# Order of the last half products, the layer sums and the turns at the end of a round, in an RWKV-6 attention with a two-layer SiLU network

## Chip, cores and metric

The kernel runs on one core of one Trainium2 chip. The metric is the device time of one execution in microseconds; lower is better.

## The reference

An RWKV-6 recurrence over 768 tokens for 4 batches and 8 heads of 48 channels gives, after a change of layout, a matrix x of 3072 x 384, which passes a network of two layers with SiLU between. All is float32.

```python
for t in range(S):
    kt, vt, rt, wt = (k[:, :, t], v[:, :, t], r[:, :, t], w[:, :, t])
    cur = np.einsum('bhd,bhe->bhde', u[None] * kt, vt)
    y[:, :, t] = np.einsum('bhd,bhde->bhe', rt, state + cur)
    state = wt[:, :, :, None] * state + np.einsum('bhd,bhe->bhde', kt, vt)
...
x = np.ascontiguousarray(attn_out.transpose(0, 2, 1, 3)).reshape(B * S, H * D)
h = x @ w_in                      # 384 -> 2048
g = h * (1.0 / (1.0 + np.exp(-h)))
return (g @ w_out).astype(np.float32)
```

## The kernel before, in words

**Tiling.** Time is cut into six chunks of 128 tokens. A *unit* is one chunk of two batches, so there are twelve units, i = 0 to 11, worked on in turn. Within a chunk the recurrence is made parallel: queries and keys are multiplied by running products of w level by level (seven levels, block sizes 1 to 64), matmuls of keys and queries give a triangle of scores, and the scores times the values, plus the queries times the state at the start of the chunk, give y. Then the state is advanced.

**A manual schedule.** Every engine works through its own instructions in the order in which the program writes them, and the program interleaves three units by hand. In the loop at line 1264, iteration i (a "round") contains

- the attention of unit i (groups of steps that `mix(i)` returns),
- the first layer of unit i-1 (`ups(i-1)`, eight steps),
- the second layer of unit i-2 (`downs(i-2)`, seven steps).

The tuple `room` says how many of the fifteen layer steps are done after each group. From unit 4 on there are eleven groups, and the last two are `end[0]` and `end[1]` in `mix`.

**The first layer** (`first_layer`, line 1049; from unit 3 on, `NFAST`) is a fast scheme: fewer products of blocks of weights and of x, with sums made beforehand. It has two halves, m = 0 and 1, of the hidden features. For each half eight named products are added up in four PSUM banks, p_h (h0, h1) and p_o (o0, o1): p1, p6, p7 and p4 in one bank, one upon the other, p5 and p3 in another, p2 and n1 in a third. After each a bank is read: ScalarE copies (line 1074), VectorE adds (line 1077), ScalarE applies SiLU (line 1080, and line 1082 for p4). The SiLU of p3 is written back to a PSUM bank, from which it is read later. In `ups` the last three steps are p7, p3 and p4 of half 1, in this order; p4 is 16 matmuls (its left operands are x sums, `spare` and `x_sum`), and each matmul leaves two records in the trace.

**The second layer** (`quarter`, line 1131) is a fast scheme of seven products Q0 to Q6, each of 8 matmuls of 128 x 192, with operands that `sums` (line 1115) makes on VectorE from the hidden features: for each half m four additions or subtractions of 128 x 512 (line 1127). Two of them read the PSUM bank that holds p3's SiLU, and the fourth reads what p4's SiLU wrote. Q0 and Q1 need no sums, Q2 to Q5 do. Q0 is written to the bank that held p3's SiLU of half 0, Q1 to the one that p4 of half 1 used. Partial results are copied by ScalarE (line 1161) before the next product may use the bank.

**The end of a round.** After the last bursts of scores (line 692) ScalarE copies eight and four blocks of them from PSUM to `score` (line 792), out of the banks p_sc and p_m. Then come, in program order:

- `turn_apart` (line 805, matmuls at 811): the keys of unit i are transposed into the p_sc banks, and `turn_k` copies them to `kq` on ScalarE (line 819). Units 10 and 11 have neither this nor the update, since no state follows them.
- `y_state` (line 826, matmuls at 835 and 842): state times queries, into the p_m banks; `y_values` (line 850): values times scores, and ScalarE's copies to `yt` (line 861).
- the turns of unit i+1 (`turn`, line 346): VectorE transposes w and k (line 360, two instructions each), and POOL makes the first product of w (`product`, line 406) between them. Turn k writes the tile that `turn_apart` of unit i reads.
- `sums` of half 0 of unit i-1.
- `update` (line 888): TensorE multiplies `kq` and values (line 896), POOL scales the state (line 901), VectorE adds (line 910).

The next round begins with the turn of r (line 360), the first growth of queries and keys (`grow_own`: POOL line 643, VectorE line 616), and the moves of x: ten DMAs from `yt` to `xt` on ScalarE's queue (line 928), two ahead of the copy of Q0's partial result and eight ahead of the next. Then POOL makes the rest of w's products (line 406), two steps of the bonus (line 491, which waits for block sums of VectorE, line 525) and the key products of levels 2 and 3 (line 634), which the next burst of scores (line 692) needs. SP issues all loads, some 60 a round.

Of the kernel before, what the change touches and what calls it, by code (L numbers as in the profile page):

```python
# [38 lines left out]
def kernel(  # L39
# [29 lines left out]
    NPAIR = 4  # L69
# [225 lines left out]
    room = pt.tile([128, 4, DM // 2], F32, name="partial", bufs=1).rearrange("p x d -> p (x d)")  # L295
# [159 lines left out]
    at = 768  # L455
# [474 lines left out]
    def both(fn, i, *args):  # L930
        return [(fn, i, b, *args) for b in range(NB)]

    def block_loads(i, names="wkr"):
        return [(load_blocks, i, name, g) for name in names for g in range(4)]
# [3 lines left out]
    def mix(i):  # L938

        ahead = i + 1 < len(units)  # L940

        def at(now, *steps):
            return steps if now else ()

        def bonus_steps(j, *steps):
            return [(block_bonus, j, x) for x in steps]

        def sum_steps(j, *steps):
            return [(block_sum, j, x) for x in steps]

        def turns(j):
            return [*both(turn, j, "w"), (product, j, 0), *both(turn, j, "k")]

        def start(j):
            return [*[(product, j, l) for l in range(1, NL)], (grow_own, j, 1)]

        end = [[*at(ahead, *bonus_steps(i + 1, 0, 1, 2, 3))],
               [*at(i < len(units) - NB, (turn_apart, i), (turn_k, i)), (y_state, i), *both(y_values, i), *at(ahead, *turns(i + 1)),
                (sums, i - 1, FH // 2 - 2 if i - 1 < NFAST else 0), *both(update, i), *at(not ahead, (move_x, i))]]
        if i < NPAIR:  # L960
            groups = [[*both(turn, i, "w"), (product, i, 0)],
                      [*both(turn, i, "k"), (odd_ones, i)], [*both(turn, i, "r"), (start_levels, i), (prepare_keys, i, 1)],
                      [(prepare, i, 1), *[(product, i, l) for l in range(1, NL)]],
                      [(burst, i, 1), (keep_level, i, 1)],
                      [(keep_level, i, 2), (go_on, i, 2)],
                      [(prepare, i, 3), (reverse_v, i), (bonus, i, 0), (bonus_sum, i, 0)],
                      [(bonus, i, 1), (burst, i, 3), (keep_level, i, 3), (bonus, i, 2)],
                      [(keep_level, i, 4), (go_on, i, 4), (bonus_sum, i, 1), (load_rk, i + 1), (load_u,)],
                      [(prepare, i, 5), (make_block_mask,), (bonus_spread, i), (bonus_write, i)],
                      [(burst, i, 5), (keep_level, i, 5), (keep_level, i, 6), (go_on, i, 6)], *end]  # L970
        else:
            groups = [[*both(turn, i, "r"), (grow_own, i, 0), (move_x, i - 1, 0, 2, nc.scalar)],
                      [*start(i), *sum_steps(i, 0, 1), *bonus_steps(i, 4, 5), (move_x, i - 1, 2, None, nc.scalar)],
                      [(odd_keys, i, 2), (grow_keys, i, 2, False), (grow_queries, i, 2), *sum_steps(i, 2)],
                      [(prepare, i, 3), *bonus_steps(i, 6, 7)],
                      [(burst, i, 3), (keep_level, i, 3), *sum_steps(i, 3, 4), (block_move, i), *at(ahead, (load_rk, i + 1))],
                      [(keep_level, i, 4), (go_on, i, 4)],
                      [(prepare, i, 5), (reverse_v, i)],
                      [(block_spread, i), (block_write, i)],
                      [(burst, i, 5), (keep_level, i, 5), (keep_level, i, 6), (go_on, i, 6)], *end]  # L980

        loads = [*at(i >= NPAIR and ahead, *block_loads(i + 1, "w")), *at(i >= NPAIR - 1 and ahead, *block_loads(i + 1, "r")),
                 *at(i + NSLOT < len(units), *block_loads(i + NSLOT, "k"))]
        if i + 1 < len(units):
            loads.insert(len(loads) // 2, (load_values, i + 1))

        if i == NPAIR - 1:
            late.extend(loads[-2:])
            loads = loads[:-2]
        if i == NPAIR:  # L990
            groups[1] += late
            groups[3] += loads[:2]
            loads = loads[2:]

        behind = groups[8 if i < NPAIR else 5 if i == NPAIR else 2:][:4 if i + NSLOT >= len(units) else None]
        for at, group in enumerate(behind):
            group += loads[at * len(loads) // len(behind):(at + 1) * len(loads) // len(behind)]
        return groups
# [3 lines left out]
    FH, DH = FC // 2, DM // 2  # L1002
    NFAST = 3
# [39 lines left out]
    def keep_banks():  # L1043

        for x in range(2):
            kept[f"h{x}"] = ps.tile([128, 512], F32, name="p_h", bufs=2)
            kept[f"o{x}"] = second[0].tile([128, 512], F32, name="p_o", bufs=2)
# [124 lines left out]
    def ups(i):  # L1172

        if i >= NFAST:
            order = (((0, "p1"), (0, "p5"), (0, "p2")), ((0, "p6"), (0, "n1"), (1, "p1")), ((0, "p7"), (0, "p3")),
                     ((0, "p4"), (1, "p2"), (1, "p6")), ((1, "p5"), (1, "n1")), ((1, "p7"),), ((1, "p3"),), ((1, "p4"),))
            made = [[(first_layer, i, half, name) for half, name in step] for step in order]
            if i == len(units) - 1:
                made[6].append((sums, i, 0))
            made[-1].append((sums, i, 1))  # L1180
            return made
        steps = [[(up, i, m)] for m in range(FC // 2)]
        for m in range(FH // 2 - (1 if i == len(units) - 1 else 2)):

            steps[FH // 2 + 1 + m].append((sums, i, m))
        steps[-1].append((sums, i, FH // 2 - 1))
        return steps

    def downs(i):
        return [[(quarter, i, x)] for x in range(7)]  # L1190

    def do(*steps):
        for fn, *args in steps:
            fn(*args)
# [69 lines left out]
    for i in range(3, len(units)):  # L1264
        steps = downs(i - 2) + ups(i - 1)
        groups = mix(i)
        if i - 1 >= NFAST:
            groups[3].append((sums_of_x, i - 1))
        if i == NTOK + 1:
            groups[4].insert(1, (weight_sums, 3))  # L1270
            for which, place in enumerate((6, 8, 9)):
                groups[place].append((in_weight_sums, which))
        if i == NFAST + 1:
            keep_banks()
            steps[1].append((in_weight_sums, 3))
        room = (1, 1, 0, 2, 1, 1, 1, 1, 1, 2, 2, 1, 1) if i < NPAIR else (2, 1, 2, 2, 1, 1, 1, 2, 1, 1, 1)
        for group, count in zip(groups, room):
            do(*group)
            for step in steps[:count]:
                do(*step)  # L1280
            steps = steps[count:]
# [34 lines left out]
```

## Time and profile before

| | |
|---|---|
| median of three runs | 594.56 us |
| the three runs | 588.8, 594.56, 597.63 us |
| span of the profiled execution | 588.6 us |
| granted TensorE clock | 1.0 throughout rounds 4 to 11 |
| TensorE busy in the chain of work that ended last | 76% of the span |

In the profile PE is a matmul, PEld a load of weights, DVE VectorE, ACT ScalarE, POOL GpSimd, SPq and ACTq the queues from which DMAs are issued. "L1065" is line 1065. A row of a timeline gives start, duration, engine, line, operation, the tile written and those read, shapes, how many instructions are merged, and in brackets how long the engine stood before and what released it. Buffer numbers are left out.

### The profile page before, as it was taken

Reading aid. Unit: us, or ns where it says so; the run is one execution under the profiler, and the core shown is the slowest. Engines: PE = TensorE matmul, PEld = TensorE weight load, DVE = VectorE, ACT = ScalarE, POOL = GpSimd, SP = SyncE. Lnnn points to the kernel's source line nnn. Section 1 sums busy time; section 2 is a strip of 40 time slices with the busy share of each in tenths; the row PEclk is TensorE's granted clock in tenths of the full one; section 3 lists DMA queues with packets and bytes.
Section 4 is the critical chain, followed back from the end, with each engine's and each line's share of the span. In section 5 each row is a group of like instructions: output and inputs, shape, how many; then the busy total and the mean of one; then the engine's idle time right before and its main releaser. Section 6 shows DMA issues by size and latency. Waiting matters only on the chain.

```text
span 588.6 us, 19384 instructions
## 1 busy us (share of the span) xinstructions
PE 573.7 (97%) x8070; PEld 533.3 (91%) x8070; DVE 455.7 (77%) x703; ACT 264.2 (45%) x582; POOL 354.1 (60%) x415
## 2 busy tenths in 40 slices
PE   8989999999999999999999999999999989999997
PEld 8767876798899989999999989999999989999997
DVE  7979789998898898787788898888678797861150
ACT  5679694431531561561561561460470462370320
POOL 5989778357768478287486496485676677500000
PEclk9999999999999999999999999999999999999999
DMA  9957785343432643544543544444354460100000
GB/s 231 311 122 195 167 244 82 47 86 70 102 68 39 133 71 53 131 66 75 114 68 60 123 62 68 105 75 73 85 100 71 95 102 27 38 7 24 28 3 26
DMA packets 203383, 53.70 MB, mean 91 GB/s; under 512 B 186784, under 2 KB 195104, under 8 KB 203296
## 3 DMA queue, kind: packets, MB, share of 16 engines
q1 hardware_dynamic: 197360, 48.73, 41.0%
q10 hardware_dynamic: 5936, 3.74, 2.4%
q8 instruction: 63, 1.03, 0.8%
q14 instruction: 24, 0.20, 0.1%
HBM read 43.21 MB, written 5.24 MB: 82 GB/s over the span
## 4 chain that ended last, share of the span: by engine, by line
PE 76%; SPq 5%; DVE 5%; POOL 4%; DMA 4%; ACT 3%; issue 1%; ACTq 1%; POOLq 0%; DVEq 0%
PE p_o L1156 26%; PE p_h L1065 16%; PE p_o L1065 8%; PE p_h L1011 8%; PE p_h L1156 4%; PE p_m L1095 4%; PE p_m L856 2%; PE p_sc L692 2%; DVE score L561 2%; SPq L127 2%; PE p_m L835 2%; DMA vq<-in_v_dram 2%; ACT score L792 2%; POOL w_in_sb L259 2%; POOL tk L634 1%
## 5 line engine op out<-in xcount | busy, mean ns | idle before, releaser
L634 POOL TENSOR_TENSOR tk<-tk,tw 128x256 f32<-128x256 f32 x128 | 91.3, 734 | 42.8 <-ACT tk L604 27.6
L491 POOL TENSOR_TENSOR ruk<-tokens_rk 128x768 f32<-128x768 f32 (+1 forms) x32 | 53.6, 1687 | 70.9 <-DVE block_sums L525 36.6
L1156 PE MATMUL p_o<-own,temps 128*128 128x192 f32 x528 | 88.8, 327 | 1.3 <-ACT partial L1161 1.3
L1156 PEld LDWEIGHTS p_o<-own,temps 128*128 128x128 f32 x528 | 86.0, 190 | 2.5 <-ACT partial L1161 2.4
L1011 PE MATMUL p_h<-xt,w_in_sb 128*128 128x256 f32 x288 | 66.1, 384 | 1.7 <-POOL w_in_sb L259 1.5
L1065 PE MATMUL p_h<-xt,w_in_sb 128*64 128x128 f32 x1008 | 62.8, 274 | 0.4 <-issue 0.4
L1011 PEld LDWEIGHTS p_h<-xt,w_in_sb 128*128 128x128 f32 x288 | 53.6, 190 | 10.0 <-POOL w_in_sb L259 2.4
L1156 PE MATMUL p_o<-w_out_sb,gt 128*128 128x192 f32 x340 | 59.9, 329 | 0.2 <-DVE temps L1127 0.2
L616 DVE TENSOR_TENSOR tr<-tr,tw 128x512 f32<-128x512 f32 x61 | 57.3, 939 | 2.6 <-PE p_m L692 2.1
L1065 PEld LDWEIGHTS p_h<-xt,w_in_sb 128*64 128x64 f32 x1008 | 55.8, 137 | 2.0 <-issue 0.9
L1156 PEld LDWEIGHTS p_o<-w_out_sb,gt 128*128 128x128 f32 x340 | 55.3, 190 | 2.0 <-issue 1.2
L1161 ACT COPY partial<-p_o 128x192 f32<-128x192 f32 x33 | 10.6, 320 | 95.7 <-PE p_o L1156 46.5
L406 POOL TENSOR_TENSOR tw<-tw 128x256 f32<-128x256 f32 (+6 forms) x83 | 40.0, 482 | 17.7 <-DVE tw L360 13.8
L1065 PE MATMUL p_o<-xt,w_in_sb 128*64 128x128 f32 x720 | 46.9, 273 | 0.0
L604 ACT COPY tk<-tk 128x256 f32<-128x256 f32 x52 | 21.2, 407 | 53.8 <-POOL tk L634 49.2
L1065 PEld LDWEIGHTS p_o<-xt,w_in_sb 128*64 128x64 f32 x720 | 40.8, 137 | 0.0
L1074 ACT COPY gt<-p_h 128x512 f32<-128x512 f32 x45 | 26.2, 582 | 30.4 <-PE p_h L1065 30.4
L1080 ACT ACTIVATE gt<-gt 128x512 f32<-128x512 f32 x36 | 22.7, 631 | 34.1 <-DVE gt L1077 33.9
L710 DVE COPY_PREDICATED score<-mask,p_sc 128x512 f32<-128x512 int8 x42 | 31.3, 800 | 5.8 <-PE p_sc L692 5.5
L1077 DVE TENSOR_TENSOR gt<-p_o,gt 128x512 f32<-128x512 f32 x27 | 18.4, 683 | 19.4 <-PE p_o L1065 19.4
L1077 DVE TENSOR_TENSOR gt<-p_h,gt 128x512 f32<-128x512 f32 x27 | 18.6, 687 | 17.3 <-PE p_h L1065 16.2
L643 POOL TENSOR_TENSOR tk<-tk,tw 128x256 f32<-128x256 f32 x32 | 30.9, 986 | 0.0
(225 smaller groups left out, 1272.0 us busy)
## 6 DMA issues: line engine op xcount, KB each, us to landing
w_out_sb<-in_moe_w_in_dram SPq DMA_DIRECT2D x6, 768.0 KB, 7.1
w_out_sb<-in_moe_w_out_dram SPq DMA_DIRECT2D x4, 768.0 KB, 5.1
own<-in_moe_w_out_dram SPq DMA_DIRECT2D x4, 768.0 KB, 5.8
tokens_rk<-in_r_dram SPq DMA_DIRECT2D x8, 384.0 KB, 4.4
tokens_rk<-in_k_dram SPq DMA_DIRECT2D x8, 384.0 KB, 5.3
tokens_w<-in_w_dram SPq DMA_DIRECT2D x8, 384.0 KB, 6.4
raw<-in_w_dram SPq DMA_DIRECT2D x80, 32.0 KB, 2.3
raw<-in_k_dram SPq DMA_DIRECT2D x80, 32.0 KB, 2.1
```

The source lines that it names most:

```text
L406: engine.tensor_tensor(out=up, in0=t[:, :, 0::2], in1=t[:, :, 1::2], op=ALU.mult)
L491: mul = lambda out, one, two: nc.gpsimd.tensor_tensor(out=out, in0=one, in1=two, op=ALU.mult)
L616: nc.vector.tensor_tensor(out=odd, in0=odd, in1=tw[i][l][:, :, 0::2][:, :, :, None].to_broadcast([128, Q, L >> (l + 1), c]), op=ALU.mult)
L634: nc.gpsimd.tensor_tensor(out=out, in0=have, in1=odd_products(i, l, b, *blocks), op=ALU.mult)
L643: nc.gpsimd.tensor_tensor(out=have, in0=have, in1=odd_products(i, l, b, [2, NP * ni]), op=ALU.mult)
L710: nc.vector.copy_predicated(out=dst, mask=masks[l][:, :, None].to_broadcast([128, NB, NP, ni, c]), data=sc[e].rearrange("p (b q) (i c) -> ...
L1011: nc.tensor.matmul(p_h[:, a, :], lhsT=w_in_sb[:, c, f * 128:(f + 1) * 128], rhs=xt[i][:, c, :], start=(c == 0), stop=(c == KC - 1))
L1065: nc.tensor.matmul(p[h:h + PD, q, :], lhsT=left[:, f:f + PD], rhs=right, start=first and n == 0 and q == 0, stop=last and n == len(pairs) ...
L1074: nc.scalar.copy(out=g(*{"p1": (0, 0), "p6": (0, 1), "p5": (1, 1)}[name]), in_=p)
L1077: nc.vector.tensor_tensor(out=to, in0=p, in1=to, op=ALU.add)
L1095: nc.tensor.matmul(po[i, b], lhsT=gt[i, f // 2][:, f % 2, b * L:(b + 1) * L], rhs=w_out_sb[:, f, :], start=(f == 0), stop=(f == FC - 1))
L1156: nc.tensor.matmul(p, lhsT=left(f), rhs=right[:, f, :], start=which in (0, 1, 3) and f == 0, stop=f == FH - 1, skip_group_check=True)
```

## The change

For rounds 4 to 11 two things are moved; no instruction is added or removed.

```diff
-        end = [[*at(ahead, *bonus_steps(i + 1, 0, 1, 2, 3))],
+        end = [[*at(i > NFAST, (sums, i - 1, 0)), *at(ahead, *bonus_steps(i + 1, 0, 1, 2, 3))],
                [*at(i < len(units) - NB, (turn_apart, i), (turn_k, i)), (y_state, i), *both(y_values, i), *at(ahead, *turns(i + 1)),
-                (sums, i - 1, FH // 2 - 2 if i - 1 < NFAST else 0), *both(update, i), *at(not ahead, (move_x, i))]]
+                *at(i <= NFAST, (sums, i - 1, FH // 2 - 2)), *both(update, i), *at(not ahead, (move_x, i))]]
...
-        room = (1, 1, 0, 2, 1, 1, 1, 1, 1, 2, 2, 1, 1) if i < NPAIR else (2, 1, 2, 2, 1, 1, 1, 2, 1, 1, 1)
+        room = (1, 1, 0, 2, 1, 1, 1, 1, 1, 2, 2, 1, 1) if i < NPAIR else (2, 1, 2, 2, 1, 1, 1, 2, 1, 2, 0)
```

`sums` of half 0 goes from behind the turns to the start of `end[0]`, ahead of p3 of half 1. The last layer step, p4 of half 1 together with `sums` of half 1, which followed `end[1]`, now follows p3 directly, ahead of `end[1]`. So the order becomes, engine by engine:

| engine | before | after |
|---|---|---|
| TensorE | p3, turn of keys, state product, values, update, p4, Q0 | p3, p4, turn of keys, state product, values, update, Q0 |
| VectorE | p7's addition, p3's addition, turns of w and k, sums 0, state, sums 1, turn of r | p7's addition, sums 0, p3's addition, sums 1, turns of w and k, state, turn of r |
| ScalarE | SiLU of p7 and p3, kq, yt, SiLU of p4, moves of x | SiLU of p7, p3 and p4, kq, yt, moves of x |

The order on POOL and of SP's DMAs stays as it is. Rounds up to 3 are unchanged.

## The prediction

> **What bounds the kernel now.** I read the page's busy times first, then a table of stretches cut at the starts of the second layer's first product (Q0, line 1156), then TensorE's waits, then the timelines of single engines around two ends of rounds. "Round i" is iteration i of the loop at line 1264; the change acts in rounds 4 to 11.
>
> ```profile
> PE 573.7 (97%) x8070; PEld 533.3 (91%) x8070; DVE 455.7 (77%) x703; ACT 264.2 (45%) x582; POOL 354.1 (60%) x415
> ```
> ```profile
> 215.40:259.60 44.20, 44.20 (x723) 43.19 (x721) 36.14 (x55) 19.37 (x47) 28.18 (x35) 1.00 0.47 85
> 304.80:351.10 46.30, 45.15 (x722) 43.43 (x720) 41.13 (x57) 19.27 (x47) 31.45 (x37) 1.00 0.45 82
> ```
> The columns of the second are the stretch, its length, and the busy us of PE, PEld, DVE, ACT and POOL, then granted clock, DMA share and GB/s. The stretch from round 5's Q0 to round 6's holds TensorE solidly and is 44.20 us long at full clock; the one from round 7 to 8 has the same matmuls and 46.30. So TensorE is the bound, and all that an order can win is the difference to 44.20 (43.20 where units lack the last products): over the eight stretches 1.3 + 0 + 1.0 + 2.1 + 0 + 1.2 + 1.9 + 0 = 7.5 us, of which the end of a round is a part.
>
> ```profile
> PE p_m L835 <- ACT score L792: 2.2, 4, 1.1
> PE p_o L1156 <- ACT partial L1161: 1.3, 2, 0.8
> ```
> ```profile
> 206.31 1.04 PE L1065 MATMUL p_h<-xt,raw 128*64 128x128 f32 x16
> 208.63 0.69 PE L811 MATMUL p_sc<-ident,tk 48*128 48x48 f32 x15 [0.21 <-ACT score L792]
> 210.18 0.96 PE L835 MATMUL p_m<-tr,state 48*48 48x128 f32 x25 [0.36 <-ACT score L792]
> ```
> ```profile
> 208.60 1.52 ACT L792 COPY score<-p_m 64x256 f32<-64x256 f32 x4
> ```
> This is the end of round 4: the turn of keys (L811) and the state product (L835) wait until ScalarE has copied scores out of the banks that they write; the L792 copies end at 210.12. The table of waits shows only part of it, because pipelined matmuls hide gaps, so I take it from starts. From the start of p3 of half 1 (206.31) to Q0 (215.39) round 4 takes 9.08 us; round 5, below, takes 251.89 to 259.58 = 7.69.
>
> ```profile
> 251.89 1.04 PE L1065 MATMUL p_h<-xt,raw 128*64 128x128 f32 x16
> 253.74 0.70 PE L811 MATMUL p_sc<-ident,tk 48*128 48x48 f32 x16
> 257.72 1.06 PE L1065 MATMUL p_h<-spare,w_in_sb 128*64 128x128 f32 x16
> 259.58 2.71 PE L1156 MATMUL p_o<-w_out_sb,gt 128*128 128x192 f32 x15
> 278.13 0.69 PE L692 MATMUL p_sc<-tr,tk 48*64 48x64 f32 x32
> ```
> The same reading gives 9.08 for round 7 (342.05 to 351.13), and 7.7 to 7.8 for rounds 6, 8 and 9. Rounds 10 and 11 have no turn of keys and no update, 0.63 + 0.72 us less, so 6.34 would be undisturbed: they take 8.31 (477.46 to 485.77) and 6.70 (522.27 to 528.97). Waits at ends of rounds: 1.39 + 1.39 + 1.97 + 0.36 = 5.1 us.
>
> **The change, part by part.** No instruction is added or removed, and SP's order is the same. *TensorE:* the 16 matmuls of p4 (32 records, 257.72 to 259.58, 1.86 us) go ahead of L811. They stand where TensorE would wait, and 1.86 covers 1.39 twice and 0.36, and all but 0.1 of 1.97: a gain of 5.0. Their inputs (x sums, weights) are long ready, but they add to the bank that VectorE reads for p7 (the L1077 before p3's), a wait that the update used to cover. That read ends at 252.87 where p4 would now start at 253.74, and in round 4 at 208.10 against 208.16: nothing, but with no room.
>
> *VectorE:* the four sums of half 0 go ahead of the addition for p3 (L1077), and the four of half 1 ahead of the turns of w and k. This is where cover may go.
>
> ```profile
> 252.18 0.69 DVE L1077 TENSOR_TENSOR gt<-p_h,gt 128x512 f32<-128x512 f32 x1 [0.72 <-PE p_h L1065]
> 253.85 0.69 DVE L1077 TENSOR_TENSOR gt<-p_h,gt 128x512 f32<-128x512 f32 x1 [0.98 <-PE p_h L1065]
> 254.46 1.30 DVE L360 STREAM_TRANSPOSE tw<-raw 128x512 f32<-128x512 f32 x2
> 257.44 0.67 DVE L1127 TENSOR_TENSOR temps<-gt,p_o 128x512 f32<-128x512 f32 x1
> 258.04 1.13 DVE L1127 TENSOR_TENSOR temps<-temps,gt 128x512 f32<-128x512 f32 x1
> ```
> In round 5's frame: half 0's sums start at 252.87 and take .57 + .60 + 1.16 + 1.21 = 3.5 us beside a busy POOL, or 4 x .60 = 2.4 beside an idle one. So p3's addition runs to 256.0 to 257.1 instead of 254.5, and its SiLU on ScalarE ends at 256.7 to 257.8. Behind that SiLU on ScalarE are p4's SiLU (0.55), the two kq copies (L819, 0.86) and the yt copies. The kq copies end at 258.1 to 259.2; the update's matmuls, now due at 257.00 + 1.86 = 258.86, wait 0 to 0.3 us. I take 0.15 in rounds 5, 6, 8 and 9. In rounds 4 and 7, where ScalarE's copies are late and TensorE now is not, the same sum gives 0.55 to 0.9; I take 0.7. Together 4 x 0.15 + 2 x 0.7 = 2.0 given back. Then yt follows 2 us later (259.2 to 261.6), and the moves of x on ScalarE's queue; the first landed in the queue at 261.01 in round 6, some later because they also wait for SP's earlier loads. The second-layer partial copy behind two moves needs Q0's end anyway, so I cost this at nothing; if that cover is gone, it is 0.8 us a round, the longest such wait shown.
>
> Half 1's sums wait for p3's SiLU (257.8 at the late end), and the fourth for p4's. With POOL idle they last 2.4 us, to 260.2; the turns of w then end at 261.5 instead of 255.76, 5.7 later. Queued behind them are the turn of k, the state addition (L910), the turn of r. Waiting for them is POOL:
>
> ```profile
> 255.84 1.04 POOL L406 TENSOR_TENSOR tw<-tw 128x512 f32<-128x512 f32 x1 [0.64 <-DVE tw L360]
> 268.78 2.41 POOL L491 TENSOR_TENSOR ruk<-tokens_rk 128x384 f32<-128x384 f32 x2 [4.31 <-DVE block_sums L525]
> 273.48 3.29 POOL L634 TENSOR_TENSOR tk<-tk,tw 128x256 f32<-128x256 f32 x4
> ```
> Its run from L406 lasts without a gap from 255.84 to 264.48, 8.64 us, then stands 4.31. After the change it is 261.55 to 270.2: the slack is eaten and the bonus step (L491) starts at 270.2, 1.4 later. VectorE's block sums are not what it waits for then, as they had the sums ahead of them before and have them ahead now. From L491's start to the last key product (273.48 + 3.29 = 276.77) it is 8.0 us, so keys are ready at 278.2, and TensorE asks for them at 278.13 (L692). That is a wait of 0.1 to 0.3, or none if half 0's sums take 2.4. I take 0.15 in each of the 7 rounds 5 to 11: 1.0 us. Bounds: 0, and 1.2 a round (8.4) should both sets of sums run at the slow rate.
>
> A rule speaks against this change. The Trainium skill, "TensorE: Matmul & The Clock Gate", section "Architectural detail", says that VectorE and ScalarE are strictly first in, first out. By it the turns pay every microsecond that a sum waits for ScalarE, as in my sum; without it the 5.7 us would be nothing. No row of this trace shows a turn passing a waiting sum.
>
> The sum: -5.0 + 2.0 + 1.0 = -2.0 us. The profiled span of 588.6 would be 586.6. The three runs have 588.8 to 597.63 and a median of 594.56, 6 us above the span: I carry the difference over and say **592.5**.
>
> **Rivals.** *All of it is kept* (chance 0.18): the sums run at 0.60 us each, nothing waits behind them, and the whole 5.0 us shows: 589.5. For: POOL stands 4.31 us. Against: its end leaves 1.4 us before L692. Even with every wait of the eight stretches gone it is 594.56 - 7.5 = 587.1, so being faster by over 2% (about what a measurement of this kernel can tell from no change: 11.9 us) needs something that no row shows: 0.02.
>
> *Slower: the keys become the bound at L692* (0.18). If the turns of w are 2 us later than I say (sums at 3.5 us twice, 2.2, on a late SiLU), the keys are at 280.2 in round 6 and TensorE stands 2.1 us in each of 7 rounds, with more waits beside: -3.0 + 7 x 2.1 = +11.7, or 606. It decides as soon as the turns end more than 5.6 us later. For: VectorE runs from 253.85 to 271 almost without rest. Against: POOL rests while the second sums run. I put 0.12 at over 2%.
>
> *Nothing is won* (0.22): the waits move from L835 to the update and to the partial copies (L1161), whose time the moves and SP's loads set; the gain of a round is lost in the next, 594 to 598.
>
> **How the numbers follow.** The forecast, -5 to +1 net, has 0.40; with the two small cases on either side 0.80, from 588 to 600. Adding the lower half of the slower case gives 588 to 602. Chances: faster 0.02, same 0.86, slower 0.12.
>
> **What would show it.** Right: in rounds 4, 7, 10 and 11 no wait of L811 and L835 for L792; p4 directly ahead of L811; turns of w 5 to 6 us later against Q0; no POOL idle ahead of L491; small new waits of L896 for L819 and of L692 for POOL. Wrong: stretches of 46 us or more in every round with L692 waiting for L634, or the old waits of L835 still there, or Q0's stretch longer because the L1161 copies come late.

## The result, and the profile after

The changed kernel takes 587.4 us (median of 9 runs, 584.72 to 588.69); the kernel before, run on the same chip in turn with it, 592.54 us (9 runs, 588.8 to 597.95). The ratio is 0.9921 with an interval of 0.9894 to 0.9949, so the change is worth 4.7 us, between 3.0 and 6.3, and the time lies below the forecast of 592.5 and just below its range, which began at 588. The profiled span went from 588.6 to 583.8 us. Rounds 4 to 11, from the first Q0 to the ninth, went from 359.06 to 354.43 us, which is 4.6 of the 4.8; what lies before and behind them did not move.

The first line is that of busy times on the page of the changed kernel, the others its stretches of rounds 5 and 7, with the same columns as before:

```profile
PE 573.1 (98%) x8070; PEld 534.3 (92%) x8070; DVE 441.4 (76%) x703; ACT 264.1 (45%) x582; POOL 354.8 (61%) x415
```
```profile
214.10:259.30 45.20, 44.70 (x724) 43.42 (x720) 35.68 (x56) 19.43 (x48) 30.44 (x35) 1.00 0.47 85
303.80:348.70 44.90, 44.71 (x722) 43.35 (x720) 35.71 (x56) 19.25 (x48) 30.10 (x35) 1.00 0.47 85
```
Round 7 lost 1.4 of its 2.1 us above 44.20; round 5, which had none, gained 1.0. So the waits were not only taken away: new ones came, also where there were none. VectorE, with as many instructions, is busy 14.3 us less: where a sum (L1127) took up to 1.24 us beside GpSimd's run in round 7, it now takes 0.68 to 0.80.

The timelines of TensorE and ScalarE at the end of round 7 show the old wait covered:

```profile
340.75 1.04 PE L1065 MATMUL p_h<-xt,raw 128*64 128x128 f32 x16
342.61 1.09 PE L1065 MATMUL p_h<-spare,w_in_sb 128*64 128x128 f32 x16
344.50 0.70 PE L811 MATMUL p_sc<-ident,tk 48*128 48x48 f32 x16
345.13 1.13 PE L835 MATMUL p_m<-tr,state 48*48 48x128 f32 x32
```
```profile
343.05 1.51 ACT L792 COPY score<-p_m 64x256 f32<-64x256 f32 x4
```
The last score copies end at 344.56, as late against p3 as they were before: they end 3.81 us after the start of p3's products (340.75 here; 210.12 against 206.31 in round 4 before). But p4 fills the 1.9 us from 342.61 to 344.50, and the state product finds its banks free. From p3 to Q0 (348.70) it is now 7.95 us instead of 9.08.

What TensorE waits for now in these rounds, from its table of waits:

```profile
PE p_h L1065 <- DVE gt L1077: 1.0, 2, 0.5
...
PE p_o L1156 <- ACT partial L1161: 0.2, 1, 0.2
```
No row of L811 or L835 is left. The first row is new: p4 waits for VectorE's addition of p7, in rounds 5 and 8. And GpSimd's run behind the turns, with the burst that needs its keys, in round 6:

```profile
260.99 1.04 POOL L406 TENSOR_TENSOR tw<-tw 128x512 f32<-128x512 f32 x1 [7.72 <-DVE tw L360]
...
268.89 2.40 POOL L491 TENSOR_TENSOR ruk<-tokens_rk 128x384 f32<-128x384 f32 x2
...
274.10 2.88 POOL L634 TENSOR_TENSOR tk<-tk,tw 128x256 f32<-128x256 f32 x4
```
```profile
277.74 0.69 PE L692 MATMUL p_sc<-tr,tk 48*64 48x64 f32 x32
```
The run starts 1.64 us after Q0, 5.4 later than before, and L491 follows without a gap, as forecast. But the keys are ready at 276.98, 0.76 ahead of the burst, and L692 never waits in rounds 4 to 11.

### The profile page after: what moved, and what is told of

Its sections match the earlier page's. It is cut to its first block, busy times and chain, and to the rows that moved or that the text cites. A ratio compares the mean times of both kernels' runs of the same rounds, so it can differ in the third digit from the quotient of the medians.

```text
span 583.8 us, 19375 instructions
## 1 busy us (share of the span) xinstructions
PE 573.1 (98%) x8070; PEld 534.3 (92%) x8070; DVE 441.4 (76%) x703; ACT 264.1 (45%) x582; POOL 354.8 (61%) x415
## 4 chain that ended last, share of the span: by engine, by line
PE 82%; DVE 5%; SPq 4%; DMA 4%; POOL 3%; issue 1%; ACT 1%; ACTq 0%; DVEq 0%; POOLq 0%
PE p_o L1156 28%; PE p_h L1065 18%; PE p_o L1065 9%; PE p_h L1011 9%; PE p_h L1156 4%; PE p_m L1095 4%; PE p_sc L692 2%; PE p_m L856 2%; DVE score L561 2%; PE p_m L835 2%; DMA vq<-in_v_dram 2%; PE p_m L692 1%; DMA raw<-in_w_dram 1%; SPq L127 1%; SPq L210 1%; POOL w_in_sb L259 1%
## 5 line engine op out<-in xcount | busy, mean ns | idle before, releaser
L634 POOL TENSOR_TENSOR tk<-tk,tw 128x256 f32<-128x256 f32 x128 | 90.4, 727 | 30.7 <-ACT tk L604 22.9
L406 POOL TENSOR_TENSOR tw<-tw 128x256 f32<-128x256 f32 (+6 forms) x83 | 40.6, 489 | 59.3 <-DVE tw L360 55.4
L491 POOL TENSOR_TENSOR ruk<-tokens_rk 128x768 f32<-128x768 f32 (+1 forms) x32 | 50.3, 1582 | 36.9 <-DMA tokens_rk<-in_k_dram 28.7
L1011 PE MATMUL p_h<-xt,w_in_sb 128*128 128x256 f32 x288 | 67.8, 391 | 0.8 <-POOL w_in_sb L259 0.6
L616 DVE TENSOR_TENSOR tr<-tr,tw 128x512 f32<-128x512 f32 x61 | 59.1, 968 | 0.9 <-PE p_m L692 0.4
L1161 ACT COPY partial<-p_o 128x192 f32<-128x192 f32 x33 | 10.5, 319 | 83.0 <-PE p_o L1156 46.6
L525 DVE TENSOR_REDUCE block_sums<-ruk 128x4 f32<-128x192 f32 (+1 forms) x48 | 24.2, 546 | 15.0 <-POOL ruk L491 14.8
L561 DVE COPY_PREDICATED score<-spare 128x1024 f32<-128x1024 int8 x16 | 34.3, 2197 | 0.3
L1077 DVE TENSOR_TENSOR gt<-p_o,gt 128x512 f32<-128x512 f32 x27 | 18.5, 684 | 20.3 <-PE p_o L1065 20.3
```

What stands on the lines that cost most here:

```text
L406: engine.tensor_tensor(out=up, in0=t[:, :, 0::2], in1=t[:, :, 1::2], op=ALU.mult)
L491: mul = lambda out, one, two: nc.gpsimd.tensor_tensor(out=out, in0=one, in1=two, op=ALU.mult)
L525: add = lambda out, have: nc.vector.tensor_reduce(out=out, in_=have, axis=mybir.AxisListType.X, op=ALU.add)
L561: nc.vector.copy_predicated(out=score[:, i % NSC, e].rearrange("p (b q) (i s) -> p b q i s", b=NB, s=BLK), mask=block_mask[:, :, None].to_ ...
L616: nc.vector.tensor_tensor(out=odd, in0=odd, in1=tw[i][l][:, :, 0::2][:, :, :, None].to_broadcast([128, Q, L >> (l + 1), c]), op=ALU.mult)
L634: nc.gpsimd.tensor_tensor(out=out, in0=have, in1=odd_products(i, l, b, *blocks), op=ALU.mult)
```

## The experiments

Sixteen runs in four groups; each group ran on one chip in turn with the kernel before. Ratios are to it. "Rounds 4 to 11" is again from Q0 to Q0 in the profiled execution.

### Which half of the change carries the gain

p4 and its SiLU ahead, all sums where they were:

```diff
-        room = (...) if i < NPAIR else (2, 1, 2, 2, 1, 1, 1, 2, 1, 1, 1)
+        room = (...) if i < NPAIR else (2, 1, 2, 2, 1, 1, 1, 2, 1, 2, 0)
...
-                (sums, ...), *both(update, i), *at(not ahead, (move_x, i))]]
+                (sums, ...), *both(update, i), *at(not ahead, (move_x, i)), *at(i > NFAST, (sums, i - 1, 1))]]
...
```
(In `ups`, left out here, the sums of half 1 no longer belong to the step of p4.)

> p4 of half 1 and its SiLU ahead of the turn of keys as in the changed kernel, all sums on VectorE at their old places. Theory T1 (cover: p4's matmuls stand where TensorE waited for the score copies): nearly the whole gain of the changed kernel, ratio 0.990 to 0.994 against the kernel before, no wait of L811 or L835 for L792 over 0.4 us, turns of w at their old place against Q0 (about -5 us) and POOL again idle ahead of L491. Theory T2 (the order on VectorE brings the gain, since POOL and VectorE collide less and the key products come on time): a ratio of 0.997 or above. Theory T3 (the gain is ScalarE's queue: the SiLU ahead of yt lets the moves of x and so the partial copies go out early): also near 0.993, and the waits of L1156 for L1161 down from 1.3 to 0.3 us or less, so the next run is needed to tell it from T1.

586.87 us, ratio 0.9903 (0.9866 to 0.9941). No wait of L811 or L835. This is all of the gain.

The same, but p4's SiLU stays at its old place on ScalarE behind the update, so that only the matmuls move:

> Only p4's matmuls of half 1 are ahead of the turn of keys; its SiLU on ScalarE and all sums stay where they were, behind the yt copies and the update. T1: 0.990 to 0.995, since the cover on TensorE is the same; L811 and L835 no longer wait, Q1 may wait up to 0.5 us a round for the SiLU that frees its bank. T2: 0.997 or above. T3: the moves of x go out as in the kernel before, the waits for L1161 are back at 1 us or more in the profile, and the ratio is 0.996 or above.

587.68 us, 0.9908 (0.9873 to 0.9943): the matmuls are the gain. The L1161 wait is 2.9 us in its table here; what that means is settled further down.

Only half 0 of the sums ahead of p3's addition, p4 at its old place:

```diff
-        end = [[*at(ahead, *bonus_steps(i + 1, 0, 1, 2, 3))],
+        end = [[*at(i > NFAST, (sums, i - 1, 0)), *at(ahead, *bonus_steps(i + 1, 0, 1, 2, 3))],
...
-                (sums, ...), *both(update, i), *at(not ahead, (move_x, i))]]
+                *at(i <= NFAST, (sums, ...)), *both(update, i), *at(not ahead, (move_x, i))]]
```


> Only the sums of half 0 are moved, ahead of p3's addition; p4, its SiLU and the sums of half 1 stay at the end of the round. T1: no gain, 0.998 to 1.004 (p3's SiLU and behind it the kq copies come 1.5 to 2.5 us later, for which the update may wait 0.3 us a round), waits of L835 for L792 as before (2 us or more). T2: 0.997 or below.

594.16 us, 1.0032 (0.9998 to 1.0065): nothing won, perhaps 2 us lost. Its table of waits has the old rows of L811 and L835, larger, and a new one:

```profile
PE p_m L835 <- ACT score L792: 2.9, 6, 1.1
...
PE p_sc L896 <- ACT kq L819: 0.7, 1, 0.7
```

The changed kernel with the turn of keys ahead of p4:

```diff
-                [..., (turn_k, i)), (y_state, i), ...
+                [..., (turn_k, i)), *at(i > NFAST, (first_layer, i - 1, 1, "p4"), (sums, i - 1, 1)), (y_state, i), ...
...
```


> The changed kernel with the turn of keys between p3 and p4: p3, turn of keys, p4, state product; the kq copies ahead of p4's SiLU on ScalarE; VectorE's order as in the changed kernel. It takes away the two new waits of the changed kernel that its profile shows: p4 for VectorE's read of p7 (1.0 us in two rounds) and the update for kq (0.2 us a round, six rounds). T1: 1 to 2 us under the changed kernel, ratio 0.988 to 0.991 against the kernel before, if the turn of keys does not wait for the first eight score copies instead (0.2 to 0.6 us a round, then no better than 0.992). T2 and T3: as the changed kernel, 0.992.

591.52 us, 0.9978 (0.994 to 1.0017). Its table of waits:

```profile
PE p_sc L811 <- POOL tokens_rk L491: 1.9, 2, 1.0
...
PE p_sc L811 <- ACT score L792: 1.5, 2, 0.8
```
The turn writes a bank that the score copies read, so it stands before them with nothing to cover it. The name in the first row is that of whatever came last by the profile; what the turn waits for in the program is the score copies and the key products, not the bonus product, and turn_split, below, takes the wait away by earlier copies alone. As long as these copies are late, p4 must stand ahead of both L811 and L835.

### Why the score copies are late at all

The slow ends of rounds in the kernel before are just those in which the block write (L561) is slow. These are VectorE's and GpSimd's timelines of round 5 in the kernel before, where nothing waits, and of round 5 in the changed kernel:

```profile
246.74 2.52 DVE L561 COPY_PREDICATED score<-spare 128x1024 f32<-128x1024 int8 x2
...
248.69 2.22 POOL L491 TENSOR_TENSOR ruk<-tokens_rk 128x768 f32<-128x768 f32 x1 [4.83 <-DMA tokens_rk<-in_k_dram]
```
```profile
245.50 5.53 DVE L561 COPY_PREDICATED score<-spare 128x1024 f32<-128x1024 int8 x2
250.92 0.68 DVE L1077 TENSOR_TENSOR gt<-p_o,gt 128x512 f32<-128x512 f32 x1
...
245.21 1.82 POOL L491 TENSOR_TENSOR ruk<-tokens_rk 128x768 f32<-128x768 f32 x1 [3.40 <-DMA tokens_rk<-in_k_dram]
247.10 2.75 POOL L491 TENSOR_TENSOR ruk<-ruk,u_bc 128x768 f32<-128x768 f32 x1
249.81 2.06 POOL L491 TENSOR_TENSOR spare<-tokens_rk 128x384 f32<-128x384 f32 x1
```
A load of the next tokens (tokens_rk) starts GpSimd's bonus products. If it lands late, the block write is over in 2.5 us; if it lands with the write, the two take turns and the write takes 4.1 to 5.8 us. Behind it on VectorE is n1's addition (L1077, in the fence at 250.92), behind that its SiLU on ScalarE, and behind that the L792 copies. Two runs ask whether this is the cause, from two sides. The first changes VectorE's order alone:

```diff
-                      [(block_spread, i), (block_write, i)],
-                      [(burst, i, 5), ...
+                      [(block_spread, i), (block_write, i, [0])],
+                      [(block_write, i, [1]), (burst, i, 5), ...
...
-        for e in range(2):
+        for e in parts:
```


> The kernel before, with VectorE's order alone changed: the second half of the block write (L561) stands behind n1's addition of p7's result (L1077) instead of ahead of it. No matmul moves. Theory A (the score copies that L811 and L835 waited for came late because n1's addition stood behind a block write that took 4 to 5.6 us beside GpSimd's bonus products instead of 2.6): the L835 and L811 waits in rounds 4, 7 and 10 (1.39, 1.39, 1.97 us) shrink to at most half, the wait of the later score products on the partial copies (L1161) shrinks too, ratio 0.992 to 0.997. Theory B (those copies are late for a reason of ScalarE's own, such as its queue of SiLU and copies): the waits stay within 20%, ratio 0.999 to 1.003. If the split only moves the delay to the burst behind it, L692 or L896 waits appear instead and the ratio is near 1.

587.06 us, 0.9915 (0.9876 to 0.9953): as much as the change, with no matmul moved, and no wait of L811 or L835 left. The L1161 wait, which was expected to shrink too, did not (3.05 us in the table below). The second leaves GpSimd's products out:

```diff
...
+        if step < 4 and i > NPAIR:
+            return
...
```


> The kernel before, leaving out GpSimd's first four groups of bonus products (L491, steps 0 to 3) in every round after the first that has them; the bonus that is written into the scores is therefore not the reference's. VectorE's and TensorE's orders are as before. Theory A (the slow block write is made by GpSimd's products that run at the same time): every L561 takes about 1.33 us, the waits at L811 and L835 in rounds 4, 7 and 10 are gone without any cover, ratio 0.989 to 0.994. Theory B (L561 is slow for its own reason, its data or its place): some L561 still take 2.9 us, the waits stay, ratio 0.998 to 1.002.

585.02 us, 0.985 (0.9813 to 0.9887). The line of the block write (L564 in this kernel, moved by three), with the least, median and longest duration in ns:

```profile
L564 DVE COPY_PREDICATED score<-spare x16: 1299/1313/1331, 201.5 to 512.8; 128x1024 f32<-128x1024 int8 x16
```
In the changed kernel the same line reads:

```profile
L561 DVE COPY_PREDICATED score<-spare x16: 1301/2680/2965, 201.1 to 514.0; 128x1024 f32<-128x1024 int8 x16
```
All sixteen are fast without the products, and the waits are gone. This kernel also does less work on GpSimd, so its time is no price of the collision alone; the mechanism is shown by both runs together.

### Do cover and cure add up

> p4's half products and their SiLU ahead of the turn of keys, the sums for the second layer where they were, and the block write split as in the run beside it. Theory A: with p4's matmuls as cover there is nothing left for the split to win at L811 and L835; only p4's own wait for p7's addition (0.5 us in all with p4 alone) can go, so the ratio is within 0.002 of p4 alone (0.988 to 0.992). Theory B: cover and earlier copies do not draw on the same waits, and the two gains add: 0.984 to 0.988.

588.73 us, 0.9943 (0.9914 to 0.9972), p4 waiting 1.5 us for p7's addition, which now stands behind the second half of the block write. They do not add: both draw on the same waits. The ratio is above both ranges that were given; that p4's longer wait (0.5 us in p4_alone) is the reason is likely, not shown.

> The changed kernel with p4 behind the turn of keys (which by itself left waits of 1 to 2 us at L811 and gave 0.998), and the block write split. Theory A: the turn of keys waited for score copies made late by the block write, so with the split L811 no longer waits, p4 stands behind and covers L835, ratio 0.987 to 0.991. Theory B: L811's wait has another cause; it stays at 1 to 2 us in two rounds or more, ratio 0.995 or above.

586.26 us, 0.9886 (0.9845 to 0.9927): with earlier copies the order that was no use (0.9978) works, L811 waits for nothing, and p4's own wait is gone too.

### How much room the keys have

```diff
-                [..., *both(y_values, i), *at(ahead, *turns(i + 1)),
-                 *at(i <= NFAST, (sums, ...)), *both(update, i), ...
+                [..., *both(y_values, i), *at(ahead and i <= NFAST, *turns(i + 1)),
+                 *at(i <= NFAST, (sums, ...)), *both(update, i), *at(ahead and i > NFAST, *turns(i + 1)), ...
```


> The changed kernel with the next turns of w and the rest that stand ahead of the update put behind it: the keys that the next round's burst products (L692) read come about 0.9 to 2 us later. This measures the margin that the prediction priced at 1.0 us. If the margin is the 0 to 0.8 us that the profile of the changed kernel shows between the last key and the burst, L692 waits 0.1 to 1.2 us in most rounds and the ratio is 0.994 to 1.002 against the kernel before. If GpSimd absorbs the delay (its idle ahead of the bonus products shrinks instead), L692 still waits for nothing and the ratio stays at 0.990 to 0.994.

587.47 us, 0.9911 (0.9876 to 0.9946), no wait at L692 in rounds 4 to 11. The turns of w end 2.79 us after Q0 instead of 1.66, and the keys still come 0.2 us ahead of the burst in round 6 (279.46 against 279.64). So another 1.1 us on VectorE was free: the keys' room is larger than the prediction had it.

### The second layer's partial copies

The L1161 copies stand on ScalarE's queue behind the issues of the moves of x, some 0.6 us each. Two runs on top of the split kernel move these away, four of them behind the copy, or eight to SyncE:

```diff
-                      [..., (move_x, i - 1, 2, None, nc.scalar)],
-                      [(odd_keys, i, 2), ..., *sum_steps(i, 2)],
+                      [..., (move_x, i - 1, 2, 6, nc.scalar)],
+                      [(odd_keys, i, 2), ..., *sum_steps(i, 2), (move_x, i - 1, 6, None, nc.scalar)],
```


> The changed kernel with p4 behind the turn of keys and the block write split, and in addition the last four moves of x (L928, issued by ScalarE at about 0.6 us each) put behind the partial copy (L1161) that the second layer's later products wait for. Theory A (that copy is late because eight issues stand ahead of it on ScalarE): the L1161 waits (2.0 us in one round of the split kernel) go, ratio 0.983 to 0.988. Theory B (ScalarE is held by the DMA that the first of the moves waits for, however many follow): the wait shrinks by less than half, ratio within 0.002 of the split kernel. If x lands too late, the first layer's first products (L1065) wait instead and the ratio is above 0.990.

585.12 us, 0.9856 (0.9813 to 0.99), the lowest ratio of a kernel that does all the work; the L1161 wait is 0.58 us.

> The same kernel with the last eight moves of x issued by SyncE instead of ScalarE. Theory A: no partial copy stands behind an issue any more, L1161 waits 0, ratio 0.982 to 0.987. Rival: SyncE's queue holds loads that wait for their buffers, the moves of x wait behind them, and the first layer waits for x at L1065 by 1 us a round or more: ratio 1.0 or above.

592.82 us, 0.9985 (0.9955 to 1.0015). No L1161 wait is left, but rounds 4 to 11 take 361.5 us. The loss that the rival named is there, but its largest rows are waits of first-layer products for ScalarE's and VectorE's readers of their banks, so how the later moves lead to them is not shown.

> The changed kernel itself, beside the others on one chip, for a comparison without the shift between chips: 0.990 to 0.994.

586.84 us, 0.9882 (0.9837 to 0.9926). But its profiled execution has a span of 589.2 us, against 583.8 for the same kernel at first. TensorE's table of waits and ScalarE's timeline of it:

```profile
PE p_o L1156 <- ACT partial L1161: 3.2, 3, 1.9
```
```profile
312.00 5.02 ACTq L928 DMA_DIRECT2D xt<-yt  x8
317.06 0.32 ACT L1161 COPY partial<-p_o 128x192 f32<-128x192 f32 x1 [7.84 <-DMA xt<-yt]
```
In round 7 the eight issues start at 312.00, 7.1 us after Q0, and the copy behind them at 317.06. By starts the products from Q2 to Q4 lose 5.66 us here, 0.46 in the first profile. Not all of it is waiting. These are the stretches in which TensorE stands and the one just behind it (the third value from the end is the granted clock):

```profile
315.60:317.40 1.80, 0.00 (x0) 0.00 (x0) 1.80 (x3) 0.34 (x2) 0.98 (x2) 1.00 0.48 87
317.70:321.10 3.40, 3.40 (x12) 3.40 (x12) 1.39 (x5) 0.21 (x1) 3.32 (x6) 0.50 0.45 64
```
Round 7 loses 3.80 us: 1.85 are the wait, and most of the rest is the clock, which is at half for the 3.4 us that follow (about 1.7 us, estimated as half of them). So a difference of a few us between two single traces can be this one wait and what follows it. The last four runs take it apart:

> The kernel before once more: ratio 1.0 within its interval. Theory A (the L811/L835 waits belong to the kernel, the L1161 wait to the execution): the waits at L811 and L835 in rounds 4 to 11 sum to 4 to 6 us again, in rounds that may differ, and the L1161 wait lies anywhere from 0 to 6 us. Theory B (both belong to the execution): L811 and L835 sum to under 3 or over 7 us.

> As the run beside it: the L811/L835 sum 4 to 6 us under theory A, under 3 or over 7 us under theory B; the L1161 wait 0 to 6 us under both.

> The changed kernel a third time: no wait at L811 and under 1 us at L835, p4's wait for p7's addition about 1 us, as in both profiles of it so far. The L1161 wait lies between 0 and 6 us; rounds 4 to 11 without it take 353.9 us within 0.5, as in both profiles so far.

> The changed kernel with the last four moves of x behind the partial copy that L1156 waits for. If the L1161 wait is worth 2 to 3 us on average in the changed kernel, as the mean over the profiles suggests (0.46 and 5.66 us), the ratio is 0.984 to 0.989 and the L1161 wait under 0.6 us; if the 5.66 us were an exception, the ratio stays at 0.989 to 0.993.

The kernel before against itself gives 1.0029 (0.9989 to 1.0069); the single times are 589.93 (before_third) and 587.46 (after_third). after_moves takes 586.24 us, 0.9912 (0.9878 to 0.9947), no better than the changed kernel: the 5.66 us were an exception. It and moves_late can't be told from the changed kernel by their intervals, so no version is shown to beat it.

The table puts the executions side by side. "Slow" is the number of rounds in which the two instructions of the block write took over 4 us together; the L1161 wait is what the three products from Q2 to Q4 take beyond 7.80 us (in after_beside with the loss by the clock in it).

| execution | slow | rounds 4-11, us | L1161 wait | without it |
|---|---|---|---|---|
| before_again | 2 | 356.98 | 1.81 | 355.17 |
| before, first | 3 | 359.06 | 2.28 | 356.78 |
| before_third | 4 | 358.73 | 0.21 | 358.52 |
| changed, first | 7 | 354.43 | 0.46 | 353.97 |
| after_beside | 4 | 359.59 | 5.66 | 353.93 |
| after_third | 4 | 355.77 | 2.06 | 353.71 |
| split_alone | 2 | 355.48 | 3.05 | 352.43 |
| no_bonus | 0 | 353.37 | 1.04 | 352.33 |

The last column is the finding. In the three executions of the kernel before it grows by about 1.7 us with every slow block write. In the changed kernel it is 353.7 to 354.0 whether four are slow or seven. Theory A held only in part: the waits at L811 and L835 are 2.7 us in before_again (1.37 in round 7, 1.35 in round 9), below the 4 to 6 it gave, because only two writes were slow, and 6.1 in before_third (1.38, 1.39, 1.37 and 1.97 in rounds 4, 6, 7 and 10), with four. Another 0.8 us in round 6 of before_again has no releaser in the trace ("issue"). These waits belong to the execution too; that they can come at all belongs to the kernel.

## Why the prediction was wrong

The sum was right in sign and in the wait that it priced. The miss is 5.1 us (592.5 against 587.4): about 1 us lies in the terms of the sum, and about 4 in the step from the sum to a time.

**The gain, -5.0.** Right, with some luck. The shortest rounds seen add up to 351.5 us (44.09 for round 4, 5 x 44.20, 2 x 43.20). The three executions of before stand 3.7, 5.3 and 7.0 above it, 5.3 on average without the L1161 wait, and p4_matmuls shows that TensorE's cover takes it. The prediction sized a quantity that depends on when a load lands from one execution with three such rounds, and that execution happened to lie in the middle.

**The kq copies, +2.0: measured 0.4.** In rounds 4, 6, 7 and 9 TensorE goes from the update (L896) to Q0 in 0.93 us, in rounds 5 and 8 in 0.82; before, it went from the update to p4 in 0.72. In p4_alone the kq copies end 0.7 us ahead of the update (212.57 against 213.26 in round 4), and it is 0.82 in all six rounds. So 0.11 in four rounds is a wait for the copies, and 0.10 in all six, 0.6 us together, is a price of the new order that the sum didn't have. The extra that I charged to rounds 4 and 7 did not come: with p4 in front TensorE reaches the update 1.9 us later there too, and ScalarE has caught up.

**The keys, +1.0: measured 0.** POOL's run from L406 to L491 lasts 7.9 us, not 8.64 (260.99 to 268.89), and starts 0.3 earlier than the 261.55 that I took in round 5's old frame (1.64 us after Q0, not 1.97). L491 starts 9.54 us after Q0 where I had 10.6. The slower rival drew on this step and fell with it; by turns_last it needs more than 1.1 us beyond the change to begin.

**p4's wait for p7's addition, 0 "but with no room": measured 1.1** (0.58 in round 5, 0.53 in round 8). These are the two rounds in which both instructions of the block write are slow, 5.5 us, so that p7's addition is late. I had read the room from rounds 4 and 5, where it was 0.06 to 0.87 us.

Together: these were charged 3.0 and come to 1.5. The new order's 0.6 is added, and 0.7 is L835 waiting 0.33 in rounds 5 and 8; rounds 10 and 11 are 0.5 shorter than any of before. That is 2.3, against the 353.9 - 351.5 = 2.4 of the table. The net by the profiles is 353.9 - 356.8 = -2.95 instead of -2.0.

**The L1161 wait, "nothing".** Nearly right, and easily misread. In the first pair of traces it is 1.8 us less, a good part of the 4.8 us by which their spans differ; over three executions each it is 1.43 before and 2.73 after, within a spread of 0.2 to 5.7 (1.7 of the largest being the clock), and after_moves wins nothing in the times. It is no effect of the change that these runs can show.

**The step that failed is the carry-over.** I took the median of three runs, 594.56, as 6 us above the traced span, called that a difference to carry over, and added all of it to the changed kernel's span of 586.6. But each execution of these two kernels whose span is known takes 1.74 to 1.86 us longer than its own span. With 1.8 in place of 6 the sum's 586.6 gives 588.4, 1.0 us above the measured time. The other 4.2 us are by how much the kernel before was slower in its median run than in the traced one. 2.0 of them were the sample: the median of the nine runs beside the changed kernel is 592.54, not 594.56. The rest is no constant that the change leaves alone. The mean granted clock is known for executions without a trace too. These are the 92 executions of the kernel before that the ratios of the experiments rest on, on four chips, and the 16 of the changed kernel:

| mean granted clock | before: executions | mean time, us | changed: executions | mean time, us |
|---|---|---|---|---|
| 0.999 or 1.0 | 23 | 589.67 | 7 | 587.07 |
| 0.996 or 0.997 | 36 | 591.52 | 9 | 587.29 |
| 0.994 or less | 33 | 594.45 | 0 | - |

At full clock the two are 2.6 us apart, which is what the profiles say (2.95) and near the sum's 2.0. Over all of them the medians are 591.81 and 587.23, 4.6 apart. So some 2 us of the gain are time that the kernel before loses at a lower clock and the changed one does not. The prediction had one trace of before, with the clock at 1.0 in all of rounds 4 to 11, and so no term for this; the low end of its range, 588, was drawn from that one trace's waits as if they were fixed.

What lowers the clock can be seen in the kept traces in part. In three of them it falls inside rounds 4 to 11, to one half for 3.4 or 6.8 us, each time right behind a place where TensorE stood for 1.8 us. One is after_beside, above. Another is sums0_alone, whose TensorE has the order of the kernel before. In its round 4 both instructions of the block write were slow (5.9 us), the score copies were late, and the turn of keys stood 1.05 and 0.77 us (on the name in the first row, see turn_first above):

```profile
209.00 0.23 PE L811 MATMUL p_sc<-ident,tk 48*128 48x48 f32 x1 [1.05 <-POOL tokens_rk L491]
210.00 0.69 PE L811 MATMUL p_sc<-ident,tk 48*128 48x48 f32 x15 [0.77 <-ACT score L792]
```
```profile
210.70:217.50 6.80, 6.63 (x106) 6.02 (x108) 3.47 (x6) 4.65 (x11) 4.36 (x7) 0.50 0.44 64
```
That round lasts 49.88 us instead of 44.09. In the changed kernel p4 stands at this place, and in its three traces TensorE waits there for 0.6 us at most. That the slower executions of before are made like this round is likely and not shown: none of them has a trace, and the longest stand in the three traced ones is 1.14 and 0.35 us, in round 10. Nor is it known when a stand lowers the clock. Four others of 1.7 to 2.4 us, one in each of moves_sp and turn_split and two in turn_first, did not.

The rival "all of it is kept" at 589.5 was the closest of the rivals in time, but for a wrong reason: not all is kept, more was there to win. "Nothing is won", by way of L1161, fell.

## What to carry to other kernels

Where an engine is bound and waits in some rounds only, ask what differs between a round that waits and one that does not before pricing the wait: here it was a load's arrival, which changes from one execution to the next, so that the wait's size in one trace is a sample. Compare each execution's time with its own span and look at its clock, not the median of some runs with the span of another: a wait may cost more than its length in executions that nobody traced. Independent work put at the waiting place took most of such a wait in every execution traced here, and moving the late producer ahead of the slow neighbour (one line on VectorE) did the same; the two do not add. Before a difference between two traces is put down to a change, look whether a second trace of the same kernel differs by as much.

## What the runs showed of the hardware

VectorE and GpSimd took turns. In the changed kernel's round 5 GpSimd's product begins at 245.21, VectorE's first L561 at 245.50; the product runs its 1.82 us, until 247.03, and L561 ends 1.2 us after that. GpSimd's next begins at 247.10 and takes 2.75 us, of which the first 1.1 are the rest of L561. The second L561 takes 2.92 us, of which the last 1.2 lie behind the end of that product; by itself one takes 1.30 to 1.33 us (no_bonus). In the kernel before L491 came later, at 248.69, and it was the product that grew (2.22 us) while L561 kept its speed.

The Trainium skill, "SBUF — State Buffer", section "Who interferes with whom", states that a VectorE instruction with two inputs in SBUF contends with a GpSimd instruction that reads SBUF, and, for VectorE's two-port modes, that whoever issues first holds the shared ports for the whole instruction while the other is fully blocked. These rows agree with both for a predicated copy with a mask and data in SBUF, an operation that the page does not list.

A product that starts 0.29 us ahead of the block write instead of 1.95 behind its start thus decides over 3.0 us of VectorE's time (5.53 against 2.52), and in the kernel before over 1.4 to 2.0 us of TensorE's in each round that it hits.

The other thing is TensorE's clock. In rounds 4 to 11 of the eighteen traces TensorE stood seven times for 1.7 to 2.4 us (two stands next to each other counted as one). Behind three of these the granted clock was 0.50 for 3.4 us, or for twice that; behind no shorter stand did it fall.
